# Single-tile x loads, matmul transposes, filler matmuls and a new load order at the start of a fused attention and SwiGLU kernel

## The chip, the cores and the metric

The kernel runs on one core of a Trainium2 chip. Its time is the device time of one execution in microseconds. The compute engines are PE (TensorE: matmuls), ACT (ScalarE), DVE (VectorE) and POOL (GpSimd); SP mainly issues transfers. All times in traces count from the start of the span; the quoted device times are about 1.7 us longer than the span. A run is called slow when it is over 1.5% above the fastest of the same kernel; such runs are left out of ratios.

## The reference, cut to what matters

```python
x = A_x                                             # 1 x 2048 x 512, bf16
g = sigmoid((x * gate_w).sum(-1, keepdims=True))
a = attention(x, wqkv)  @ wo                        # 32 heads of 16, causal, window of 256
b = (silu(x @ w1) * (x @ w3)) @ w2                  # F = 1376
return g * a + (1 - g) * b
```

## The kernel before

The kernel computes one static order for all engines from assumed durations and assumed landing times of the loads (the numbers in `dma(...)`), and then emits its instructions in that order. An engine works through its instructions in this order: when one waits for a load, everything behind it on that engine waits too (PE does so for 2.60 us below). A "burst" is a group of score matmuls, followed by an exp on ACT. `gate_w` is loaded as one extra column of `w1`, so that the sum for the gate comes out of the FFN matmuls.

```python
    dma("x0", "SP", 4.1, lambda: x_dma(0, 0))        # 256 tokens in one transfer
    dma("k0", "ACT", 3.6, lambda: w_dma(nc.scalar, wk_sb, A_wqkv, 0, P, D))
    dma("x1", "SP", 4.9, lambda: x_dma(0, 1))
    dma("q0", "ACT", 4.2, lambda: w_dma(nc.scalar, wq_sb, A_wqkv, 0, P))
    dma("v", "SP", 6.5, lambda: w_dma(nc.sync, wv_sb, A_wqkv, 0, D, 2 * D))
    dma("x2", "SP", 7.3, lambda: x_dma(1, 0))
    dma("x3", "SP", 8.0, lambda: x_dma(1, 1))
    dma("kq", "SP", 10.5, ...)                       # K/Q weights of the later heads
    dma("wa", "SP", 13.8, ...)                       # first part of w1 and w3
    ...                                              # [cut: x by DMA transpose, wb, w2]
    nc.gpsimd.dma_start(out=w1_sb[:, :, F:F + 1],    # gate_w: 512 elements of 2 bytes
                        in_=gate_w.rearrange("(c p x) -> p c x", p=P, x=1))
    ...
                        nc.tensor.transpose(out=tx[:, j, c, :], in_=xs_tiles[m2][:, j, d0:d0 + P],
                                            identity=ident[:])      # into bf16 PSUM
    ...
    T0, PACE, NWARM = 4.0, 2.55, 6                   # six dummy matmuls in front
```

The softmax here doesn't subtract the row's maximum and nothing guards it: scores larger than these inputs give would overflow.

Of the kernel before, what the change touches and what calls it, by code (L numbers as in the profile page):

```python
# [7 lines left out]
ALU = mybir.AluOpType  # L8
ACT = mybir.ActivationFunctionType
BF16 = mybir.dt.bfloat16  # L10
# [5 lines left out]
P = 128  # L16
# [3 lines left out]
def kernel(  # L20
# [80 lines left out]
    nc.vector.memset(scr[:], 0.0)  # L101
    xs_tiles = {}

    def x_dma(t, h):
        xs = xp.tile([P, 2, D], BF16, name=f"xs{2 * t + h}")
        nc.sync.dma_start(
            out=xs[:],
            in_=x2d[512 * t + 256 * h:512 * t + 256 * (h + 1), :].rearrange("(m p) d -> p m d", p=P))
        xs_tiles[2 * t + h] = xs

    def xt_dma(t, c):
        nc.sync.dma_start_transpose(out=xT[:, c, 512 * t:512 * (t + 1)],
# [2 lines left out]
    def w_dma(eng, dst, src, lo, hi, base=0):  # L115
        eng.dma_start(out=dst[:, :, lo:hi],
                      in_=src[:, base + lo:base + hi].rearrange("(c p) f -> p c f", p=P))
# [2 lines left out]

    land = {}

    def dma(name, eng, at, fn):
        fn()
        land[name] = at

    dma("x0", "SP", 4.1, lambda: x_dma(0, 0))
    dma("k0", "ACT", 3.6, lambda: w_dma(nc.scalar, wk_sb, A_wqkv, 0, P, D))
    dma("x1", "SP", 4.9, lambda: x_dma(0, 1))
    dma("q0", "ACT", 4.2, lambda: w_dma(nc.scalar, wq_sb, A_wqkv, 0, P))  # L130
    dma("v", "SP", 6.5, lambda: w_dma(nc.sync, wv_sb, A_wqkv, 0, D, 2 * D))
    dma("x2", "SP", 7.3, lambda: x_dma(1, 0))
    dma("x3", "SP", 8.0, lambda: x_dma(1, 1))
    dma("kq", "SP", 10.5, lambda: (w_dma(nc.sync, wk_sb, A_wqkv, P, D, D),
                                   w_dma(nc.sync, wq_sb, A_wqkv, P, D)))
    FA = 4 * P
    dma("wa", "SP", 13.8, lambda: (w_dma(nc.sync, w1_sb, B_w1, 0, FA),
                                   w_dma(nc.sync, w3_sb, B_w3, 0, FA)))
    dma("x4", "SP", 20.0, lambda: [xt_dma(2, c) for c in range(NDC)])
    dma("wb", "SP", 24.0, lambda: (w_dma(nc.sync, w1_sb, B_w1, FA, F),  # L140
                                   w_dma(nc.sync, w3_sb, B_w3, FA, F)))
    dma("x6", "SP", 30.0, lambda: [xt_dma(3, c) for c in range(NDC)])
    dma("w2", "SP", 34.0, lambda: (
        nc.sync.dma_start(out=w2_sb[:, 0:NFC - 1, :],
                          in_=B_w2[0:(NFC - 1) * P, :].rearrange("(f p) n -> p f n", p=P)),
        nc.sync.dma_start(out=w2_sb[0:FL, NFC - 1, :], in_=B_w2[(NFC - 1) * P:F, :])))
    wo_t = []

    def wo_dma():
        for j in range(2):  # L150
            wo_t.append(xp.tile([P, 2, D], BF16, name=f"xs{j}"))
            nc.sync.dma_start(out=wo_t[j][:], in_=A_wo[256 * j:256 * (j + 1), :].rearrange(
                "(c p) n -> p c n", p=P))

# [6 lines left out]
                            compare_op=ALU.is_ge, fill=0.0, base=0, channel_multiplier=1)  # L161
    nc.gpsimd.affine_select(out=eo[:], in_=eo[:], pattern=[[2 * DH, 4]],
                            compare_op=ALU.is_ge, fill=0.0, base=DH - 1, channel_multiplier=-1)
    nc.vector.tensor_reduce(out=maskEO[:, 0:1], in_=eo[:], axis=mybir.AxisListType.X, op=ALU.add)
    nc.vector.tensor_scalar(out=maskEO[:, 1:2], in0=maskEO[:, 0:1], scalar1=-1.0, scalar2=1.0,
                            op0=ALU.mult, op1=ALU.add)
    nc.gpsimd.dma_start(out=w1_sb[:, :, F:F + 1], in_=gate_w.rearrange("(c p x) -> p c x", p=P, x=1))
    nc.gpsimd.memset(Vaug[:, :, :, DH:DH + 1], 1.0)
    nc.scalar.activation(out=scr[:, 1:2], in_=scr[:, 0:1], func=ACT.Tanh)

# [23 lines left out]

    xT_op = {}

    def add_tx(m2):
        xT_op[m2] = []
        for half in range(2):
            key = ("tx", m2, half)  # L200
            hold("g", key, 1)
            cs = slice(2 * half, 2 * half + 2)

            def pe(key=key, half=half):
                tx = bank(key, BF16, (P, 2, 2, P))
                for j in range(2):
                    for c in range(2):
                        d0 = (2 * half + c) * P
                        nc.tensor.transpose(out=tx[:, j, c, :], in_=xs_tiles[m2][:, j, d0:d0 + P],
                                            identity=ident[:])  # L210

            def evac(eng, key=key, cs=cs):
                dst = xT[:, cs, 2 * m2 * P:(2 * m2 + 2) * P].rearrange("p c (j t) -> p j c t", j=2)
                if eng == "ACT":
                    nc.scalar.copy(out=dst, in_=g_tile[key][:])
                else:
                    nc.vector.tensor_copy(out=dst, in_=g_tile[key][:])

            a = Op("PE", 0.25 if m2 > 1 else 0.45, pe, [loads[f"x{m2}"]], acq=[("g", key)], kind="tx")
            xT_op[m2].append(Op("ACT" if half else "DVE", 0.55 if half else 0.36, evac, [a],  # L220
                                rel=[("g", key)], rank=-1))

    def xdep(t0, t1):
        r = []
        for m2 in range(t0 // 256, (t1 + 255) // 256):
            r += xT_op[m2] if m2 < 4 else [loads["x4" if m2 < 6 else "x6"]]
        return r

    qk_tile = {}
# [105 lines left out]
    def add_up(t, f):  # L335
        fs = fsz(f)
        has_z = f == NFC - 1
        kg, ku, kt_, kh = ("G", t, f), ("U", t, f), ("tt", t, f), ("h1", t, f)
        hold("g", kg, 2)
        hold("g", ku, 1)  # L340
        hold("tt", kt_, 1)
        hold("h1", kh, 1)
        if f == 0:
            hold("hT", t, 4)
        tl = {}

        def pe(key, wsb, d0):
            m = fs + 1 if has_z and key == kg else fs

            def fn():  # L350
                b = bank(key) if d0 == 0 else g_tile[key]
                for dc in range(d0, d0 + 1):
                    nc.tensor.matmul(b[0:m, :], lhsT=wsb[:, dc, f * P:f * P + m],  # L353
                                     rhs=xT[:, dc, t * 512:(t + 1) * 512],
                                     start=(dc == 0), stop=(dc == NDC - 1))
            return fn

        def th(eng):
            m = fs
            if has_z:  # L360
                tl["tt"] = xp.tile([P, 512], F32, name="xs2")
                m = fs + 1
            else:
                tl["tt"] = sb.tile([P, 512], BF16, name=f"tt{slot('tt', kt_)}")
            nc.scalar.activation(out=tl["tt"][0:m, :], in_=g_tile[kg][0:m, :], func=ACT.Tanh,
                                 scale=0.5)

        def s1(eng):
            tl["h1"] = sb.tile([P, 512], BF16, name=f"h1_{slot('h1', kh)}")
            nc.vector.scalar_tensor_tensor(out=tl["h1"][0:fs, :], in0=tl["tt"][0:fs, :], scalar=1.0,  # L370
                                           in1=g_tile[kg][0:fs, :], op0=ALU.add, op1=ALU.mult)

        def s2(eng):
            if t not in h_tile:
                h_tile[t] = sb.tile([P, NFC, 512], BF16, name=f"hT{slot('hT', t)}")
            nc.vector.tensor_tensor(out=h_tile[t][0:fs, f, :], in0=tl["h1"][0:fs, :],
                                    in1=g_tile[ku][0:fs, :], op=ALU.mult)

        w = loads["wa" if f < 4 else "wb"]
        x = xdep(512 * t, 512 * (t + 1))  # L380
        a0, a = pe_unit(0.87, [pe(kg, w1_sb, i) for i in range(NDC)], x + [w], acq=[("g", kg)],
                        kind="ffn")
        u0, u = pe_unit(0.87, [pe(ku, w3_sb, i) for i in range(NDC)], x + [w], acq=[("g", ku)],
                        kind="ffn")
        b = Op("ACT", 0.55, th, [a], rel=[("g", kg)], acq=[("tt", kt_)], rank=0.3)
        d = Op("DVE", 0.68, s1, [b], rel=[("g", kg), ("tt", kt_)], acq=[("h1", kh)])
        e = Op("DVE", 0.68, s2, [d, u], rel=[("g", ku), ("h1", kh)],
               acq=[("hT", t)] if f == 0 else [])
        up_done.setdefault(t, []).append(e)
        if has_z:  # L390
            add_gate(t, b, tl, fs)
        return [a0, u0]
# [175 lines left out]
        pv_out[(c, p)] = Op("SP", 2.6, tr, [b])  # L568
        return a0

    T0, PACE, NWARM = 4.0, 2.55, 6
    SEQ = []
    for p in range(NP):
        SEQ += [("d", 2 * p), ("d", 2 * p + 1)] + ([("f", p)] if p < NP - 1 else [])
# [11 lines left out]
                return n  # L586
        return per_c

    for m2 in range(4):
        add_tx(m2)  # L590
    for c in range(NDC):
        pieces = [(0, 256), (256, 512)] if c == 0 else [(0, 512)]
        pieces += [(512 * t, 512 * t + 512) for t in range(1, NTC)]
# [37 lines left out]
                d.users.append(o)  # L631
    left = {o: sum(isinstance(d, Op) for d in o.deps) for o in ops}
    free_at = {e: 0.0 for e in ("PE", "ACT", "DVE", "POOL", "SP")}
    free_at["PE"] = 3.9
    ready = {e: [] for e in free_at}
    slots = {p: [(0.0, i) for i in range(n)] for p, n in SLOTS.items()}
    count = dict(refs)
# [95 lines left out]
                    ready[x].append(u)  # L733

    with tc.manual_schedule():
        b = ps.tile([P, 512], F32, name="g0")
        for i in range(NWARM):
            nc.tensor.matmul(b[:], lhsT=warm[:, 0:P], rhs=warm[:], start=(i == 0),  # L738
                             stop=(i == NWARM - 1))
        for o in order:  # L740
            if o.kind == "burst" and not wo_t:
                wo_dma()
            if o.eng == "PE":
                o.fn()
            else:
                o.fn(o.eng)
# [30 lines left out]
```

## Time and profile before

| | |
|---|---|
| device time, 6 runs | 263.51 us median (261.43 to 264.49) |
| device time, 40 runs in the rounds with the change | 263.04 us median (260.54 to 264.98) |
| profiled execution | 263.83 us, span 262.1 us |
| last matmul ends | 258.5 us |
| PE idle, waiting for V's weights | 2.60 us at 8.0 |

The page of the kernel before starts with the span, then lists busy time, share of the span and instructions of each engine (the line goes on with the other engines):

```profile
span 262.1 us, 6553 instructions
PE 253.5 (97%) x2750; PEld 124.6 (48%) x2750; DVE 150.5 (57%) x266; ACT 195.1 (74%) x143; POOL 150.2 (57%) x251
```

PE sets the time, and whatever delays PE's stream at the start delays the end by the same amount (the second table under a3 shows it). The timeline of PE around its one large wait, kernel before. Columns: start and length in us, engine, source line, operation, output and inputs, shape, count; in brackets the idle time just before and what ended it.

```profile
5.94 1.06 PE L249 MATMUL g_165<-xT,wq_sb 128*128 128x256 bf16 x4
6.79 0.79 PE L249 MATMUL g_171<-xT,wk_sb 128*128 128x256 bf16 x4
7.42 0.60 PE L249 MATMUL g_177<-xT,wq_sb 128*128 128x256 bf16 x4
10.62 1.03 PE L294 MATMUL g_184<-edm_91,xT 128*128 128x512 bf16 x2 [2.60 <-DMA edm_91<-in_A_wqkv_dram]
11.59 0.61 PE L483 MATMUL big<-qz_164,kt_163 32*128 32x512 bf16 x4
12.14 1.03 PE L294 MATMUL g_184<-edm_91,xT 128*128 128x512 bf16 x2
```

`edm_91` holds V's weights. The first V projection starts at 10.62, after 2.60 us of nothing. The same kernel in the table of windows (busy time of PE in each stretch, granted TensorE clock, share of the DMA engines, GB/s):

```profile
core 0: us, PE busy (x), PEclk, DMA share, GB/s
6.00:8.00 2.00, 2.00 (x14) 1.00 0.79 247
8.00:10.60 2.60, 0.03 (x1) 1.00 1.08 358
10.60:14.00 3.40, 3.38 (x18) 0.50 1.10 346
14.00:20.00 6.00, 6.00 (x66) 1.00 1.29 155
```

After the idle stretch the clock is halved for one record of 3.4 us: 128x512 matmuls then start 400 to 427 ns apart instead of 215 to 216. The third view is the DMA traffic from 4 to 7 us, kernel before, in 40 slices of 75 ns (tenths of the 16 engines' time, GB/s), then packets and bytes of each queue: q1 is SP's, q10 ACT's, q0 the software queue, which carries only gate_w here.

```profile
DMA  9999999995914560240014336561854344858599
GB/s 427 362 324 290 287 280 280 277 198 123 56 24 1 1 2 0 1 1 0 27 68 109 123 109 164 150 125 68 97 109 123 137 164 150 218 177 246 205 233 233
q1 hardware_dynamic: 325, 0.32, 33.6%
q10 hardware_dynamic: 525, 0.13, 19.4%
q0 software_dynamic: 24, 0.00, 11.4%
```

From 4.8 us the engines move almost nothing, and then under 250 GB/s, although V's transfer was issued at 1.82 us.

### The profile page before, as it was taken

What the parts mean: (1) busy time and instruction counts of PE and PEld (TensorE: products, weight loads), DVE (VectorE), ACT (ScalarE), POOL (GpSimd) and SP (SyncE); (2) the same over time, 40 slices, a digit from 0 to 9 for tenths busy, and PEclk for the clock granted to TensorE, in tenths of its full rate; (3) what the DMA queues carried; (4) which work ended last, traced back from release to release, by engine and by line L of the source; (5) the groups of instructions that cost most, each with busy time, mean ns of one, the idle gap of its engine ahead of it and who ended that gap; (6) DMA issues with size and microseconds to landing.
All of it is one profiled execution on the core that took longest, in us unless ns stands there. A gap on an engine that the chain in (4) does not pass through costs nothing.

```text
span 262.1 us, 6553 instructions
## 1 busy us (share of the span) xinstructions
PE 253.5 (97%) x2750; PEld 124.6 (48%) x2750; DVE 150.5 (57%) x266; ACT 195.1 (74%) x143; POOL 150.2 (57%) x251
## 2 busy tenths in 40 slices
PE   7699999999999999999999999999999999998994
PEld 4253555544554455544454555554554454434551
DVE  2267665848647456746656458456467557446353
ACT  3287978778888887888879787798788787788400
POOL 6037575556746667556755757555756666556700
PEclk9899999999999999999999999999999999999999
DMA  5999930100000000000000000000000211101111
GB/s 140 340 177 292 318 49 9 14 10 13 11 13 10 13 10 3 13 10 13 11 13 13 11 8 10 9 10 13 14 10 13 50 48 50 41 17 54 53 50 40
DMA packets 26869, 13.05 MB, mean 50 GB/s; under 512 B 18292, under 2 KB 26836, under 8 KB 26840
## 3 DMA queue, kind: packets, MB, share of 16 engines
q1 hardware_dynamic: 25752, 12.38, 19.6%
q8 instruction: 21, 0.34, 0.6%
q10 hardware_dynamic: 1056, 0.26, 0.4%
q0 software_dynamic: 32, 0.00, 0.1%
q14 instruction: 8, 0.07, 0.1%
HBM read 7.38 MB, written 2.11 MB: 36 GB/s over the span
## 4 chain that ended last, share of the span: by engine, by line
PE 89%; DMA 5%; ACT 2%; issue 1%; DVE 1%; SPq 1%; ACTq 0%
PE big L483 11%; DMA edm_91<-in_A_wqkv_dram 3%; DMA OT<-ocur 2%; PE g_1331 L406 1%; PE g_3059 L406 1%; PE g_2201 L406 1%; PE g_4040 L406 1%; PE g_3406 L406 1%; PE g_1623 L406 1%; PE g_3188 L406 1%; PE g_2468 L406 1%; PE g_1856 L406 1%; PE g_1469 L406 1%; PE g_3683 L406 1%; PE g_2710 L406 1%; PE g_2317 L406 1%
## 5 line engine op out<-in xcount | busy, mean ns | idle before, releaser
L353 PEld LDWEIGHTS <-w_sb 128*128 128x128 bf16 (+2 forms) x352 | 31.6, 100 | 38.3 <-issue 9.1
L294 PEld LDWEIGHTS <-xT 128*128 128x128 bf16 x64 | 5.8, 98 | 9.4 <-DMA edm_91<-in_A_wqkv_dram 2.9
L434 PEld LDWEIGHTS <-OT 128*128 128x128 bf16 x64 | 5.8, 97 | 8.5 <-issue 1.5
L483 PE MATMUL big<-qz_2678,kt_2677 32*128 32x512 bf16 (+1 forms) x120 | 9.0, 329 | 0.8 <-ACT edm_3937 L491 0.6
L249 PEld LDWEIGHTS <-wq_sb 128*128 128x128 bf16 x68 | 6.5, 100 | 6.1 <-issue 0.2
L483 PE MATMUL big<-qz_164,kt_163 32*128 32x512 bf16 (+1 forms) x120 | 9.2, 336 | 0.0
L249 PEld LDWEIGHTS <-wk_sb 128*128 128x128 bf16 x68 | 6.1, 99 | 6.3 <-issue 1.1
L483 PE MATMUL big<-qz_722,kt_721 32*128 32x512 bf16 (+1 forms) x120 | 9.0, 329 | 0.0
L483 PE MATMUL big<-qz_1724,kt_1723 32*128 32x512 bf16 (+1 forms) x120 | 9.0, 329 | 0.0
L483 PEld LDWEIGHTS <-kt_2677 32*128 32x128 bf16 x120 | 2.6, 91 | 8.3 <-issue 8.0
L500 POOL TENSOR_SCALAR_AFFINE_SELECT edm_200<-edm_200 128x512 bf16<-128x512 bf16 x2 | 1.2, 645 | 9.2 <-ACT edm_200 L491 9.2
L406 PEld LDWEIGHTS <-hT_355 128*128 128x128 bf16 (+1 forms) x44 | 4.0, 98 | 5.2 <-issue 1.1
L406 PEld LDWEIGHTS <-hT_2989 128*128 128x128 bf16 (+1 forms) x44 | 4.1, 97 | 4.6
L406 PEld LDWEIGHTS <-hT_1310 128*128 128x128 bf16 (+1 forms) x44 | 3.9, 97 | 4.9 <-issue 0.9
L406 PEld LDWEIGHTS <-hT_2134 128*128 128x128 bf16 (+1 forms) x44 | 3.9, 97 | 4.7 <-issue 0.7
L483 PEld LDWEIGHTS <-kt_163 32*128 32x128 bf16 x120 | 2.4, 91 | 7.6 <-issue 7.4
L483 PEld LDWEIGHTS <-kt_721 32*128 32x128 bf16 x120 | 2.4, 91 | 7.0 <-issue 6.8
L483 PEld LDWEIGHTS <-kt_1723 32*128 32x128 bf16 x120 | 2.4, 91 | 6.9 <-issue 6.8
L491 ACT ACTIVATE edm_200<-big 128x2048 bf16<-128x2048 f32 x1 | 1.9, 1877 | 4.3 <-PE big L483 4.3
L294 PE MATMUL g_184<-edm_91,xT 128*128 128x512 bf16 x4 | 2.1, 620 | 2.6 <-DMA edm_91<-in_A_wqkv_dram 2.6
L738 PE MATMUL g_133<-warm 128*128 128x512 bf16 x6 | 2.7, 630 | 1.3 <-DVE scr L101 1.3
L505 POOL TENSOR_SCALAR_AFFINE_SELECT ef_2464<-ef_2464 128x512 bf16<-128x512 bf16 x4 | 2.4, 637 | 1.4 <-ACT ef_2464 L491 1.4
(896 smaller groups left out, 948.9 us busy)
## 6 DMA issues: line engine op xcount, KB each, us to landing
out_dram<-ot SPq DMA_DIRECT2D x16, 128.0 KB, 1.7
w_sb<-in_B_w_dram SPq DMA_DIRECT2D x2, 864.0 KB, 8.0
w_sb<-in_B_w_dram SPq DMA_DIRECT2D x1, 1280.0 KB, 6.6
w_sb<-in_B_w_dram SPq DMA_DIRECT2D x2, 512.0 KB, 8.2
OT<-ocur SPq DMA_TRANSPOSE x64, 2.3
edm_91<-in_A_wqkv_dram SPq DMA_DIRECT2D x1, 512.0 KB, 8.8
wk_sb<-in_A_wqkv_dram SPq DMA_DIRECT2D x1, 384.0 KB
wq_sb<-in_A_wqkv_dram SPq DMA_DIRECT2D x1, 384.0 KB, 10.2
```

What stands on the lines that cost most here:

```text
L249: nc.tensor.matmul(b[:, 0:n], lhsT=(wq_sb if is_q else wk_sb)[:, dc, c * P:(c + 1) * P], rhs=xT[:, dc, t0:t1], start=(dc == 0), stop=(dc = ...
L294: nc.tensor.matmul(b[:], lhsT=xT[:, c, m * P:(m + 1) * P], rhs=wv_sb[:, c, :], start=(c == 0), stop=(c == NDC - 1))
L353: nc.tensor.matmul(b[0:m, :], lhsT=wsb[:, dc, f * P:f * P + m], rhs=xT[:, dc, t * 512:(t + 1) * 512], start=(dc == 0), stop=(dc == NDC - 1))
L406: nc.tensor.matmul(b[:], lhsT=h_tile[t][0:fs, f, (m % 4) * P:(m % 4 + 1) * P], rhs=w2_sb[0:fs, f, :], start=(f == 0), stop=(f == NFC - 1))
L434: nc.tensor.matmul(b[:], lhsT=OT[:, c * S + m * P:c * S + (m + 1) * P], rhs=wo_t[c // 2][:, c % 2, :], start=(c == 0), stop=(c == NDC - 1))
L483: nc.tensor.matmul(big[:, u, k * 256:k * 256 + 2 * w], lhsT=kt[32 * u:32 * u + 32, kb * P:(kb + 1) * P], rhs=qz[32 * u:32 * u + 32, :, q0: ...
L491: nc.scalar.activation(out=e[:, :, 0:2 * n], in_=tl["big"][:, :, 0:2 * n], func=ACT.Exp, scale=SCALE)
L500: nc.gpsimd.affine_select(out=tri, in_=tri, pattern=[[0, 2], [0, 2], [1, P]], compare_op=ALU.is_ge, fill=0.0, base=0, channel_multiplier=-1)
L505: nc.gpsimd.affine_select(out=tri, in_=tri, pattern=[[0, 4], [-1, P]], compare_op=ALU.is_ge, fill=0.0, base=-1, channel_multiplier=1)
L738: nc.tensor.matmul(b[:], lhsT=warm[:, 0:P], rhs=warm[:], start=(i == 0), stop=(i == NWARM - 1))
```

## The change

The intent: begin the transposes as soon as the first 128 tokens have landed; keep PE busy until the rest lands (fillers, and transposes done as ordinary matmuls with the identity into fp32 PSUM); and take from the crowded start what is needed only later (gate_w, the K/Q weights of later heads).

```diff
-    def x_dma(t, h):
-        xs = xp.tile([P, 2, D], BF16, name=f"xs{2 * t + h}")
+    def x_dma(m0, n):
+        xs = xp.tile([P, n, D], BF16, name=f"xs{m0}")
 ...
+    dma("x0", 3.0, lambda: x_dma(0, 1))
+    dma("k0", 4.0, lambda: w_dma(nc.scalar, wk_sb, A_wqkv, 0, P, D))
+    dma("x1", 3.6, lambda: x_dma(1, 1))
+    dma("q0", 4.4, lambda: w_dma(nc.scalar, wq_sb, A_wqkv, 0, P))
+    dma("x2", 4.7, lambda: x_dma(2, 2))
+    dma("v", 6.6, lambda: w_dma(nc.sync, wv_sb, A_wqkv, 0, D, 2 * D))
+    dma("x4", 7.4, lambda: x_dma(4, 2))
+    dma("x6", 8.1, lambda: x_dma(6, 2))
+    dma("wa", 11.4, ...)           # kq now stands behind x12, before w2
 ...
-    nc.gpsimd.dma_start(out=w1_sb[:, :, F:F + 1], in_=gate_w...)   # now gate_dma(), at the 8th burst
-    nc.vector.tensor_reduce(out=maskEO[:, 0:1], ...)               # now three small ops on POOL
 ...
-    nc.tensor.transpose(out=tx[:, j, c, :], in_=..., identity=ident[:])
+    nc.tensor.matmul(tx[:, c - c0, :], lhsT=xs_tiles[m][:, c * P:(c + 1) * P],
+                     rhs=ident[:], start=True, stop=True)
+    if m < 2 and c1 == NDC:
+        warm_up(1 + m)             # one filler behind tile 0, two behind tile 1
 ...
-    T0, PACE, NWARM = 4.0, 2.55, 6
+    T0, PACE, NWARM = 4.0, 2.55, 4
 ...                                # [cut: evacuations in halves for tiles 0 and 1; wo also at the 8th burst]
```

More of the change, by code (lines that the diff above doesn't have):

```diff
@@ L102 @@
     xs_tiles = {}
-    def x_dma(t, h):
-        xs = xp.tile([P, 2, D], BF16, name=f"xs{2 * t + h}")
+    def x_dma(m0, n):
+        xs = xp.tile([P, n, D], BF16, name=f"xs{m0}")
         nc.sync.dma_start(
-            out=xs[:],
-            in_=x2d[512 * t + 256 * h:512 * t + 256 * (h + 1), :].rearrange("(m p) d -> p m d", p=P))
-        xs_tiles[2 * t + h] = xs
+            out=xs[:], in_=x2d[P * m0:P * (m0 + n), :].rearrange("(m p) d -> p m d", p=P))
+        for j in range(n):
+            xs_tiles[m0 + j] = xs[:, j, :]
     def xt_dma(t, c):
@@ L121, with dma @@
     land = {}
-    def dma(name, eng, at, fn):
+    def dma(name, at, fn):
         fn()
         land[name] = at
-    dma("x0", "SP", 4.1, lambda: x_dma(0, 0))
-    dma("k0", "ACT", 3.6, lambda: w_dma(nc.scalar, wk_sb, A_wqkv, 0, P, D))
-    dma("x1", "SP", 4.9, lambda: x_dma(0, 1))
-    dma("q0", "ACT", 4.2, lambda: w_dma(nc.scalar, wq_sb, A_wqkv, 0, P))
-    dma("v", "SP", 6.5, lambda: w_dma(nc.sync, wv_sb, A_wqkv, 0, D, 2 * D))
-    dma("x2", "SP", 7.3, lambda: x_dma(1, 0))
-    dma("x3", "SP", 8.0, lambda: x_dma(1, 1))
-    dma("kq", "SP", 10.5, lambda: (w_dma(nc.sync, wk_sb, A_wqkv, P, D, D),
-                                   w_dma(nc.sync, wq_sb, A_wqkv, P, D)))
-    FA = 4 * P
-    dma("wa", "SP", 13.8, lambda: (w_dma(nc.sync, w1_sb, B_w1, 0, FA),
-                                   w_dma(nc.sync, w3_sb, B_w3, 0, FA)))
-    dma("x4", "SP", 20.0, lambda: [xt_dma(2, c) for c in range(NDC)])
-    dma("wb", "SP", 24.0, lambda: (w_dma(nc.sync, w1_sb, B_w1, FA, F),
-                                   w_dma(nc.sync, w3_sb, B_w3, FA, F)))
-    dma("x6", "SP", 30.0, lambda: [xt_dma(3, c) for c in range(NDC)])
-    dma("w2", "SP", 34.0, lambda: (
+    dma("x0", 3.0, lambda: x_dma(0, 1))
[6 more added lines that the diff above has]
+    dma("x6", 8.1, lambda: x_dma(6, 2))
+    FA = 4 * P
+    dma("wa", 11.4, lambda: (w_dma(nc.sync, w1_sb, B_w1, 0, FA),
+                             w_dma(nc.sync, w3_sb, B_w3, 0, FA)))
+    dma("x8", 17.0, lambda: [xt_dma(2, c) for c in range(NDC)])
+    dma("wb", 23.0, lambda: (w_dma(nc.sync, w1_sb, B_w1, FA, F),
+                             w_dma(nc.sync, w3_sb, B_w3, FA, F)))
+    dma("x12", 28.0, lambda: [xt_dma(3, c) for c in range(NDC)])
+    dma("kq", 31.0, lambda: (w_dma(nc.sync, wk_sb, A_wqkv, P, D, D),
+                             w_dma(nc.sync, wq_sb, A_wqkv, P, D)))
+    dma("w2", 35.0, lambda: (
         nc.sync.dma_start(out=w2_sb[:, 0:NFC - 1, :],
@@ L147, with gate_dma @@
     wo_t = []
+    def gate_dma():
+        nc.gpsimd.dma_start(out=w1_sb[:, :, F:F + 1],
+                            in_=gate_w.rearrange("(c p x) -> p c x", p=P, x=1))
     def wo_dma():
         for j in range(2):
-            wo_t.append(xp.tile([P, 2, D], BF16, name=f"xs{j}"))
+            wo_t.append(xp.tile([P, 2, D], BF16, name=f"xs{2 * j + 2}"))
             nc.sync.dma_start(out=wo_t[j][:], in_=A_wo[256 * j:256 * (j + 1), :].rearrange(
@@ L163 @@
                             compare_op=ALU.is_ge, fill=0.0, base=DH - 1, channel_multiplier=-1)
-    nc.vector.tensor_reduce(out=maskEO[:, 0:1], in_=eo[:], axis=mybir.AxisListType.X, op=ALU.add)
-    nc.vector.tensor_scalar(out=maskEO[:, 1:2], in0=maskEO[:, 0:1], scalar1=-1.0, scalar2=1.0,
+    nc.gpsimd.tensor_tensor(out=eo[:, 0:2], in0=eo[:, 0:2], in1=eo[:, 2:4], op=ALU.add)
+    nc.gpsimd.tensor_tensor(out=maskEO[:, 0:1], in0=eo[:, 0:1], in1=eo[:, 1:2], op=ALU.add)
+    nc.gpsimd.tensor_scalar(out=maskEO[:, 1:2], in0=maskEO[:, 0:1], scalar1=-1.0, scalar2=1.0,
                             op0=ALU.mult, op1=ALU.add)
-    nc.gpsimd.dma_start(out=w1_sb[:, :, F:F + 1], in_=gate_w.rearrange("(c p x) -> p c x", p=P, x=1))
     nc.gpsimd.memset(Vaug[:, :, :, DH:DH + 1], 1.0)
@@ L195, with warm_up, add_tx, pe @@
     xT_op = {}
-    def add_tx(m2):
-        xT_op[m2] = []
-        for half in range(2):
-            key = ("tx", m2, half)
-            hold("g", key, 1)
-            cs = slice(2 * half, 2 * half + 2)
-            def pe(key=key, half=half):
-                tx = bank(key, BF16, (P, 2, 2, P))
-                for j in range(2):
-                    for c in range(2):
-                        d0 = (2 * half + c) * P
-                        nc.tensor.transpose(out=tx[:, j, c, :], in_=xs_tiles[m2][:, j, d0:d0 + P],
-                                            identity=ident[:])
-            def evac(eng, key=key, cs=cs):
-                dst = xT[:, cs, 2 * m2 * P:(2 * m2 + 2) * P].rearrange("p c (j t) -> p j c t", j=2)
+    def warm_up(n):
+        b = ps.tile([P, 4, 512], F32, name="big")
+        for i in range(n):
+            nc.tensor.matmul(b[:, 0, :], lhsT=warm[:, 0:P], rhs=warm[:], start=(i == 0),
+                             stop=(i == n - 1))
+    def add_tx(m):
+        xT_op[m] = []
+        halves = [(0, 2), (2, 4)] if m < 2 else [(0, 4)]
+        for n, (c0, c1) in enumerate(halves):
+            key = ("tx", m, c0)
+            hold("g", key, 1)
+            def pe(key=key, c0=c0, c1=c1):
+                tx = bank(key, shape=(P, c1 - c0, P))
+                for c in range(c0, c1):
+                    nc.tensor.matmul(tx[:, c - c0, :], lhsT=xs_tiles[m][:, c * P:(c + 1) * P],
+                                     rhs=ident[:], start=True, stop=True)
+                if m < 2 and c1 == NDC:
+                    warm_up(1 + m)
+            def evac(eng, key=key, c0=c0, c1=c1):
+                dst = xT[:, c0:c1, m * P:(m + 1) * P]
                 if eng == "ACT":
@@ L217, in evac @@
                     nc.vector.tensor_copy(out=dst, in_=g_tile[key][:])
-            a = Op("PE", 0.25 if m2 > 1 else 0.45, pe, [loads[f"x{m2}"]], acq=[("g", key)], kind="tx")
-            xT_op[m2].append(Op("ACT" if half else "DVE", 0.55 if half else 0.36, evac, [a],
-                                rel=[("g", key)], rank=-1))
+            src = loads[f"x{m if m < 2 else m - m % 2}"]
+            a = Op("PE", (0.11 if m < 4 else 0.058) * (c1 - c0) + 0.43 * (1 + m) * (m < 2 and c1 == NDC), pe, [src], acq=[("g", key)],
+                   kind="tx")
+            on_act = n == 1 or (len(halves) == 1 and m % 2 == 1)
+            xT_op[m].append(Op("ACT" if on_act else "DVE", 0.36 if len(halves) == 2 else 0.66, evac,
+                               [a], rel=[("g", key)], rank=-1))
     def xdep(t0, t1):
         r = []
-        for m2 in range(t0 // 256, (t1 + 255) // 256):
-            r += xT_op[m2] if m2 < 4 else [loads["x4" if m2 < 6 else "x6"]]
+        for m in range(t0 // P, (t1 + P - 1) // P):
+            r += xT_op[m] if m < 8 else [loads["x8" if m < 12 else "x12"]]
         return r
@@ L360, in th @@
             if has_z:
-                tl["tt"] = xp.tile([P, 512], F32, name="xs2")
+                tl["tt"] = xp.tile([P, 512], F32, name="xs6")
                 m = fs + 1
@@ L587, in first_use @@
         return per_c
-    for m2 in range(4):
-        add_tx(m2)
+    for m in range(8):
+        add_tx(m)
     for c in range(NDC):
@@ L633 @@
     free_at = {e: 0.0 for e in ("PE", "ACT", "DVE", "POOL", "SP")}
-    free_at["PE"] = 3.9
+    free_at["PE"] = 3.0
     ready = {e: [] for e in free_at}
@@ L735 @@
     with tc.manual_schedule():
-        b = ps.tile([P, 512], F32, name="g0")
-        for i in range(NWARM):
-            nc.tensor.matmul(b[:], lhsT=warm[:, 0:P], rhs=warm[:], start=(i == 0),
-                             stop=(i == NWARM - 1))
+        warm_up(NWARM)
         for o in order:
-            if o.kind == "burst" and not wo_t:
+            if o is burst_ops[7]:
                 wo_dma()
+                gate_dma()
             if o.eng == "PE":
```

## The prediction

> **What bounds the kernel.** TensorE. The page gives PE 97% of a 262.1 us span; the table of windows shows PE 40.0 of every 40 us from 20 to 180; the chain of waits is 89% PE. ACT is busy 74%, DVE 57%, POOL 57%. Time without PE is at the ends: 3.6 us of draining after the last matmul (258.5), about 1 us of small waits between 220 and 250, and the start.
>
> **The start (timeline of PE, windows).** Six dummy matmuls 1.26 to 4.00, transposes from 4.15, first Q/K projections to 8.02, then PE stands still 2.60 us until V's weights land (10.58; issued 1.82, 8.76 us on the way). The groups name that DMA as the releaser. Then the granted clock is 0.50 from 10.6 to 13.9: 128x512 matmuls start 427 ns apart there, 216 ns afterwards. The Trainium skill, "TensorE: Matmul & The Clock Gate", Part 1, says that an idle window of about 3.4 us halves the clock; this trace agrees (one 3.41 us record at 0.5 after the stall). Loss: half of 3.3 us = 1.65. Matmuls before about 7.1 us also run at the slow spacing; that stays.
>
> Why V is late: all DMA engines go nearly empty from 4.6 to 5.5 and carry 50 to 250 GB/s until 7, then 340 to 370. In that stretch the 32 packets of the software queue (gate_w, 2-byte elements) run[...]. The skill's "DMA: Bandwidth & Descriptors", Specifications, says that transfers under 512 B are read-modify-write, below line rate. I think gate_w holds the engines up; the trace shows coincidence, not cause.
>
> **What the change does.**
> - It removes gate_w from the start. The bytes ahead of V are the same 768 KB, so V should land about 7 (estimate: 768 KB done by 5.0 as now, 512 KB at 340 GB/s = 1.5 us, plus 0.4): the 2.6 us stall mostly goes, and the slow-clock window, 1.65 us. Sum about 4.2.
> - The first x tile is half the size: transposes start near 3.1, not 4.15 (-1.05). But three fillers at 427 ns now stand behind it (+1.28). Net +0.2 to +0.4.
> - Transposes become ordinary matmuls with fp32 results: same 107/56 ns spacing, but evacuating 512 columns rises from 0.41 to about 0.69 us on DVE (as for V). Those engines have room.
> - K/Q weights of later heads move behind x and FFN weights: FFN weights land about 2 us sooner; later heads need theirs only after 35 us. Off the critical path. wo and gate_w move to the eighth burst, needed much later.
> - After about 18 us the PE stream is the same work, shifted; the static order is recomputed, perhaps ±0.5 us.
>
> Gain: 2.6 + 1.65 - 0.4 - 0.5 (leftover stalls on V or FFN weights) = about 3.3 us: 263.5 becomes 260.2 us, 1.3% less. Range 258.3 to 262.3. Chances: faster by over 2% 0.12, within 2% 0.86, slower 0.02.
>
> **What would show it.** PE timeline: no wait over 0.5 us on V's weights; V landing at 6.5 to 7.5; no clock record of 0.5 after 7 us; transposes from about 3.1; first burst at 7.5 to 8.5, not 11.6; first FFN matmul (19.7 now) about 3 us earlier; steady state unchanged; DMA not empty near 5 us.
>
> **What would make it wrong.** V still late because descriptors, not gate_w, open the gap (gain then 1 to 2 us); FFN weights landing after the schedule's 11.4 and stalling PE; POOL blocked by the gate_w issue in the middle of the masks; or a clock window so phased that the start warms up sooner (gain up to 5 us).

## The result, and the profile after

| | before | after |
|---|---|---|
| median | 263.04 us (40 runs) | 261.49 us (20 runs) |
| range | 260.54 to 264.98 | 260.91 to 264.31 |
| ratio of fast runs | | 0.9978, 95% interval 0.9954 to 1.0003: the same |
| profiled execution | 263.83 us | 260.30 us |

A ratio is the mean time of one kernel's fast runs over that of the other's of the same rounds, so it is not quite the ratio of the medians. The time lies inside the predicted range, but the forecast was a gain of 1.3% and the measured one is 0.2%. Three later samples of the same kernel gave 0.9963, 0.9935 and 0.993, so the gain is somewhere between 0.2 and 0.7%, still about half of the forecast at best.

The profile of after seemed to say the opposite. Its page, its timeline of PE and its windows:

```profile
span 258.6 us, 6559 instructions
```

```profile
5.93 0.48 PE L218 MATMUL g_166<-ident,xs_98 128*128 128x128 bf16 x4
6.25 0.60 PE L263 MATMUL g_174<-xT,wq_sb 128*128 128x256 bf16 x4
6.68 0.60 PE L263 MATMUL g_180<-xT,wk_sb 128*128 128x256 bf16 x4
7.16 0.82 PE L308 MATMUL g_186<-edm_91,xT 128*128 128x512 bf16 x3
7.91 0.40 PE L497 MATMUL big<-qz_173,kt_172 32*128 32x512 bf16 x4
```

```profile
8.00:10.60 2.60, 2.27 (x25) 1.00 1.09 359
10.60:14.00 3.40, 3.40 (x21) 1.00 1.15 179
```

There is no wait for V, no halved clock, and the span is 3.5 us shorter than that of before. Both profiles are single draws, though: before's execution (263.83) was 0.9 us slower than its mean of 262.92, and after's (260.30) was faster than every one of the 20 timed runs. Two profiles from opposite sides of two scatters made 3.5 us out of a difference of 0.8 us between the means.

### The profile page after: what moved, and what is told of

The parts are those of the page before. It is cut to its first block, busy times and chain, and to the rows that moved or that the text cites. A ratio compares the mean times of both kernels' runs of the same rounds, so it can differ in the third digit from the quotient of the medians.

```text
span 258.6 us, 6559 instructions
## 1 busy us (share of the span) xinstructions
PE 252.0 (97%) x2751; PEld 123.9 (48%) x2751; DVE 150.4 (58%) x265; ACT 195.3 (76%) x144; POOL 150.7 (58%) x254
## 4 chain that ended last, share of the span: by engine, by line
PE 87%; ACT 6%; POOL 2%; issue 1%; DVE 1%; DMA 1%; SPq 0%; POOLq 0%; ACTq 0%
PE big L497 11%; PE g_4064 L420 1%; PE g_3417 L420 1%; PE g_3988 L420 1%; PE g_3684 L420 1%; PE g_3200 L420 1%; PE g_2465 L420 1%; PE g_2153 L420 1%; PE g_2719 L420 1%; PE g_2337 L420 1%; PE g_1483 L420 1%; PE g_1335 L420 1%; PE g_1853 L420 1%; PE g_1619 L420 1%; PE g_4093 L420 1%
## 5 line engine op out<-in xcount | busy, mean ns | idle before, releaser
L263 PEld LDWEIGHTS <-wq_sb 128*128 128x128 bf16 x68 | 5.9, 97 | 5.9 <-issue 1.4
L205 PE MATMUL big<-warm 128*128 128x512 bf16 x7 | 3.6, 629 | 1.3 <-DVE scr L101 1.3
L514 POOL TENSOR_SCALAR_AFFINE_SELECT edm_203<-edm_203 128x512 bf16<-128x512 bf16 x2 | 1.2, 643 | 5.7 <-ACT edm_203 L505 5.7
L519 POOL TENSOR_SCALAR_AFFINE_SELECT ef_654<-ef_654 128x512 bf16<-128x512 bf16 x4 | 2.4, 634 | 1.5 <-ACT ef_654 L505 1.5
L519 POOL TENSOR_SCALAR_AFFINE_SELECT ef_2484<-ef_2484 128x512 bf16<-128x512 bf16 x4 | 2.4, 635 | 1.4 <-ACT ef_2484 L505 1.4
L519 POOL TENSOR_SCALAR_AFFINE_SELECT ef_279<-ef_279 128x512 bf16<-128x512 bf16 x4 | 2.4, 635 | 1.4 <-ACT ef_279 L505 1.4
```

The source lines that it names most:

```text
L205: nc.tensor.matmul(b[:, 0, :], lhsT=warm[:, 0:P], rhs=warm[:], start=(i == 0), stop=(i == n - 1))
L263: nc.tensor.matmul(b[:, 0:n], lhsT=(wq_sb if is_q else wk_sb)[:, dc, c * P:(c + 1) * P], rhs=xT[:, dc, t0:t1], start=(dc == 0), stop=(dc = ...
L514: nc.gpsimd.affine_select(out=tri, in_=tri, pattern=[[0, 2], [0, 2], [1, P]], compare_op=ALU.is_ge, fill=0.0, base=0, channel_multiplier=-1)
L519: nc.gpsimd.affine_select(out=tri, in_=tri, pattern=[[0, 4], [-1, P]], compare_op=ALU.is_ge, fill=0.0, base=-1, channel_multiplier=1)
```

## The experiments

All kernels gave correct results. Each was timed in five rounds beside the kernel before on its own chip; four kernels went to a chip together, so the groups below (a1, a2, e1, e2; e3 to e6; e7 to e9 with a3; f1, f2, f4, a4) share a chip and its runs of before. The result raised two theories: A, that V's lateness in before is a matter of luck, and B, that it is there in every execution and the change gives its value back elsewhere.

### a1, a2: both kernels again

> The kernel before, unchanged. Ratio 1.000 to itself within 0.3%. Its times should fall again in two groups, near 261.5 and near 263.6. Theory A (the late V is a matter of luck: gate_w's small packets delay V only in some executions, and the profile of before fell in one): a second profile shows V landing at another time, a stall between 0 and 2.6 us, and a profile of the 261.5 group has a stall under 1 us. Theory B (V is late in every execution of before, and the two groups come from the phase of the clock window): V lands at 10 to 11 us again, stall 2.3 to 2.9 us, whatever the group.

Measured: ratio 0.9963 (interval 0.9906 to 1.002); before against itself and just outside the expected 0.3%, so this is the size of the noise. The profile (262.99 us) shows a wait for V of 1.82 us instead of 2.60, V at 9.94, and again a halved clock. V and the wait fall just short of what B expected (10 to 11, 2.3 to 2.9 us) and inside A's wider range, so this run alone decides nothing.

Theory B put the two groups of times down to the clock, and the record bears it out. Each run lists its mean clock, and one halved record of 3.41 us takes about 0.0065 off a mean over 262 us (estimate: half of 3.41 over 262). Of the 50 runs of before in these experiments, 21 list 0.997 or more (mean 261.82 us), 24 list 0.991 to 0.993 (263.46) and five 0.985 or 0.986 (264.92); the first two groups overlap a little (up to 262.81, from 262.61). So a halved record costs about 1.6 us, and 21 of 50 executions had none.

> The kernel after, unchanged. Ratio to before 0.997 +- 0.002. Both theories: no wait for V, V landing near 7. Theory A: a profile of its slower group (263.5) would show some other wait or slow clock at the start of about 2 us. Theory B: the slower group shows the clock going full one or two windows later, with no wait.

Measured: 261.66 us, 0.9963 (0.9912 to 1.0013). The profile has waits where the first one had none: 0.57 us for x tiles 2 and 3, 0.36 us for V, which landed at 8.46. The first part of the expectation, V near 7, failed.

### e1: only gate_w moves

```diff
 # before
-    nc.gpsimd.dma_start(out=w1_sb[:, :, F:F + 1], in_=gate_w...)
 ...
+            if o is burst_ops[7]:
+                nc.gpsimd.dma_start(out=w1_sb[:, :, F:F + 1], in_=gate_w...)
```

> Before, with only the load of gate_w moved from the start to the eighth burst. Theory A: V lands at 6.5 to 7.5 in the profile, times mostly in the 261.5 group, ratio 0.995 to before. Theory B: the same landing, but ratio 0.984 to 0.990 (stall and slow window gone in every execution), so faster than the whole change, which then gives about 2 us back elsewhere (fillers, fp32 evacuations, order). Rival C (gate_w has nothing to do with it, the gap comes from descriptors): V still lands after 9.5, ratio 1.000.

Measured: 259.66 us (259.35 to 260.03), 0.9873 (0.9827 to 0.9919). One moved load is 3.3 us faster than before (means 259.65 and 262.98) and 2.4 us faster than the whole change on that chip (262.01). The timeline of PE of e1, same columns as above:

```profile
5.92 1.06 PE L248 MATMUL g<-xT,wq_sb 128*128 128x256 bf16 x4
6.77 0.70 PE L248 MATMUL g<-xT,wk_sb 128*128 128x256 bf16 x4
7.31 0.60 PE L248 MATMUL g<-xT,wq_sb 128*128 128x256 bf16 x4
7.75 0.59 PE L293 MATMUL g<-edm,xT 128*128 128x512 bf16 x2
```

This is the stream of before without the hole. Nor is the clock halved (windows, columns as above):

```profile
8.00:10.60 2.60, 2.49 (x26) 1.00 1.11 330
10.60:14.00 3.40, 3.40 (x28) 1.00 1.15 330
```

The DMA traffic from 4 to 7 us in e1 has no hole either:

```profile
DMA  9999999999999999989999999999999999999999
GB/s 393 335 311 287 304 260 287 311 317 321 287 283 273 232 246 246 341 259 369 369 328 341 300 369 369 341 355 314 369 341 369 328 355 341 369 341 369 341 355 301
```

The trace also keeps the semaphore updates of each transfer. The Trainium skill, "DMA: Bandwidth & Descriptors", section "Why a DMA increments its semaphore by 16 and not by 1", says that each engine that takes part in a transfer adds its own 1 when its data is there; the traces agree, with 16 updates for every load at the start. So one can see how far apart the engines finish (us; the updates of each transfer in order of time, since the trace does not name the engines):

| transfer | first | 8th | 15th | last |
|---|---|---|---|---|
| gate_w, before | 5.98 | 6.66 | 7.97 | 9.14 |
| V, before | 7.48 | 8.04 | 9.32 | 10.58 |
| x behind V, before | 8.18 | 8.76 | 10.05 | 11.32 |
| V, e1 | 6.73 | 6.89 | 7.05 | 7.10 |

In before, V's arrivals follow gate_w's at 1.3 to 1.8 us, from the first to the last, as if each engine had to end its share of gate_w before its share of V; the spread of 3.1 us is handed on to the next transfer. Without gate_w the sixteen arrivals lie within 0.37 us. That gate_w is the cause, where the prediction had only a coincidence, is shown by the moved load; how the two queues share an engine is read from the order of the arrivals alone. Nor is it shown what in this load holds the engines up. Its own packets took only 11.4% of the engines' time in the view of 4 to 7 us above; for most of the hole the trace shows the engines doing nothing. Its sixteen packets of 64 bytes took 185 to 775 ns each in before, and 44 ns each when e1 ran the same load at 29 us. e1 moved the 2-byte pieces and the software queue together; gate_w on SP's or ACT's queue at the start would have told them apart, and was not run.

### e2: the change with gate_w put back

```diff
 # after
+    gate_dma()
     nc.gpsimd.memset(Vaug[:, :, :, DH:DH + 1], 1.0)
 ...
                 wo_dma()
-                gate_dma()
```

> After, with only the load of gate_w put back at the start. Theory A: V late in some executions only, ratio 0.999 to before. Theory B: V lands after 9.5, a stall of 2 us or more, ratio 1.005 to 1.010 (slower than before by the fillers). Rival C: V lands near 7 as in after, ratio 0.997.

Measured: 265.03 us, 1.0073 (1.0024 to 1.0123), slower than before. V landed at 10.13; already x tiles 2 and 3 were late (8.02), PE waited 2.56 us for them, and the clock was halved afterwards. Timeline of PE of e2:

```profile
8.06 0.62 PE L219 MATMUL g<-ident,xs 128*128 128x128 bf16 x8 [2.56 <-DMA xs<-in_A_x_dram]
8.52 0.95 PE L264 MATMUL g<-xT,wq_sb 128*128 128x256 bf16 x4
```

Theory B holds (every run of before was slower than every run of e1): gate_w is worth 3 us from either side, and everything else in the change together costs about 2.

### e3 to e6: one part of the rest undone at a time

No sample of after ran on this chip, so "like after" compares ratios to before with those of other chips.

Fillers all in front, as before (the order stays that of after):

```diff
 # after
-                if m < 2 and c1 == NDC:
-                    warm_up(1 + m)
-    T0, PACE, NWARM = 4.0, 2.55, 4
+    T0, PACE, NWARM = 4.0, 2.55, 6
```

> After, with the three fillers behind tiles 0 and 1 taken out and six dummy matmuls at the front as before (order otherwise the same). The question is where the change gives back the 2.2 us by which before with gate_w moved alone (259.66) beats it (about 261.9). Theory F (fillers stand in the critical PE stream, 3 x 427 ns): ratio to before 0.991 to 0.993, about 1.2 us faster than after. Theory D (x tiles 2 and 3 and V land later than with paired loads): PE just waits where the fillers stood, ratio 0.996 to 0.998, within 0.4 us of after, wait for x of 1 us or more in the profile.

Measured: 261.83 us, 0.9968 (0.9925 to 1.001), like after. PE stood where the fillers had been, waiting for x tiles 2 and 3. Timeline of PE of e3:

```profile
3.79 1.06 PE L218 MATMUL g<-ident,xs 128*128 128x128 bf16 x8
6.91 0.62 PE L218 MATMUL g<-ident,xs 128*128 128x128 bf16 x8 [2.06 <-DMA xs<-in_A_x_dram]
```

Tiles 0 and 1 in one transfer:

```diff
 # after
-    dma("x0", 3.0, lambda: x_dma(0, 1))
+    dma("x0", 3.0, lambda: x_dma(0, 2))
-    dma("x1", 3.6, lambda: x_dma(1, 1))
+    land["x1"] = 3.6
+    dma("x2", 4.7, lambda: x_dma(2, 2))     # moved here from behind q0
```

> After, with tiles 0 and 1 loaded in one transfer as before, tiles 2 and 3 issued right behind it (one issue earlier). Static order the same as after. Theory D: tiles 2 and 3 land by about 5, V by 7.8, no wait for x over 0.2 us after the fillers, ratio 0.988 to 0.991, and the slower group of after near 263.5 disappears. Theory F: no better than after, 0.996 to 1.000 (the first transposes start 0.7 us later).

Measured: 261.96 us, 0.9962 (0.9919 to 1.0005), like after, so theory D alone failed. Tiles 2 and 3 did land early (5.21), but now the fillers stood in front of their transposes. Timeline of PE of e4:

```profile
5.26 1.06 PE L205 MATMUL big<-warm 128*128 128x512 bf16 x2
6.11 0.99 PE L218 MATMUL g<-ident,xs 128*128 128x128 bf16 x8
6.94 0.60 PE L263 MATMUL g<-xT,wq_sb 128*128 128x256 bf16 x4
```

Transposes as before (bf16 results), instruction for instruction the same order:

```diff
 # after
-                tx = bank(key, shape=(P, c1 - c0, P))
+                tx = bank(key, BF16, (P, c1 - c0, P))
-                    nc.tensor.matmul(tx[:, c - c0, :], lhsT=..., rhs=ident[:], start=True, stop=True)
+                    nc.tensor.transpose(out=tx[:, c - c0, :], in_=..., identity=ident[:])
```

> After, with PE transposes into bf16 in place of matmuls with the identity into fp32, everything else the same instruction for instruction. Theory M (the fp32 evacuations delay the projections): evacuations of 512 columns fall from 0.69 to 0.42 us on DVE, the 0.21 us wait for xT goes, ratio 0.003 or more below after's 0.9965. Theories D and F: within 0.15% of after. If transposes do not count as activity for the clock, the clock would be granted later and the kernel up to 1 us slower.

Measured: 261.41 us, 0.9957 (0.991 to 1.0005). The 0.21 us wait for xT went, as expected; the time is not distinguishable from after's. The first clock record, at full speed, begins at 5.5 us, within the 4.5 to 7.0 of the four profiles of after, so no delay of the clock by transposes showed.

K/Q weights of the later heads in front of the FFN weights again:

```diff
 # after
+    dma("kq", 31.0, ...)    # moved back up, before wa
```

> After, with the K/Q weights of the later heads issued before the FFN weights again, as in before. Compute order the same as after. Theories D and F: within 0.2% of after (0.9965), because those weights stand behind x and V either way and the FFN weights, about 2 us later (near 14), are first used at 17 to 18.6 us. If FFN weights were what after waits for, this would be slower by 1 us or more.

Measured: 261.30 us, 0.9943 (0.9901 to 0.9985), not distinguishable from after. No wait for FFN weights appeared in its profile.

### e7, e8, e9: the two delays together, and the load sizes

e7 is e3 and e4 in one.

> After, with both undone at once that changed nothing each alone: tiles 0 and 1 in one transfer, and no fillers behind the tiles (six dummy matmuls in front). In e3 the first projection waited for x tiles 2 and 3 (7.37), in e4 for the fillers (6.94). Theory J (two events in parallel delay the first projection, and taking one away uncovers the other): the first projection starts near 6.0, ratio to before 0.988 to 0.991, most of the 2.2 us back. Rival S (the recomputed static order is what costs): projection near 6.0 but ratio still 0.995 to 0.997.

Measured: 260.66 us, 0.9914 (0.9871 to 0.9956), against 261.23 for after on the same chip. The first projection starts at 5.65, as theory J wanted, but only about 0.5 us came back (means 260.75 and 261.22). Now PE waited 1.53 us for V: it asked for V at 6.69 and V landed at 8.18 (this profile fell on e7's slowest run). Timeline of PE of e7:

```profile
8.22 0.82 PE L306 MATMUL g<-edm,xT 128*128 128x512 bf16 x3 [1.53 <-DMA edm<-in_A_wqkv_dram]
```

e8 moves the Q weights of the first heads from the ACT queue to the SP queue:

```diff
 # after
-    dma("q0", 4.4, lambda: w_dma(nc.scalar, wq_sb, A_wqkv, 0, P))
     dma("x2", 4.7, lambda: x_dma(2, 2))
+    dma("q0", 4.4, lambda: w_dma(nc.sync, wq_sb, A_wqkv, 0, P))
```

> After, with the Q weights of the first heads moved from the ACT queue to the SP queue, behind x tiles 2 and 3. Theory D2 (with x in small transfers the SP queue runs short, so that the ACT queue's weights take the engines first and x tiles 2 and 3 land late): x tiles 2 and 3 land before 5.5, no wait for x, first projection at 6.2 to 6.5, V 7.2 to 8; ratio 0.989 to 0.993. If the late x has another cause: x still lands after 6, ratio 0.996.

Measured: 261.50 us, 0.9941 (0.9899 to 0.9984), like after. Tiles 2 and 3 landed at 5.73, inside after's own range (5.43 to 6.30) and later than in three of its four profiles, and V at 8.47. Theory D2, that the ACT queue's weights push x back, is not supported.

e9 takes e1 and cuts its first two x loads into four:

```diff
 # e1
-        nc.sync.dma_start(out=xs[:], in_=x2d[...256 rows...].rearrange("(m p) d -> p m d", p=P))
+        for j in range(2):                   # for the first 512 tokens only
+            r = 512 * t + 256 * h + P * j
+            nc.sync.dma_start(out=xs[:, j, :], in_=x2d[r:r + P, :])
```

> e1 (before with gate_w late, 259.66, ratio 0.987), with the first two x loads each cut into two transfers of one token tile; nothing else, compute order the same. Theory D2: tiles 2 and 3 land 0.5 to 1.5 us later than e1's 5.1, the first projection starts near 6.4 to 7.2 instead of 5.9, ratio 0.990 to 0.994, with more spread. If cutting the loads is harmless: ratio 0.987 as e1, spread 0.7 us.

Measured: 261.23 us (260.46 to 261.92), 0.9934 (0.9893 to 0.9974), against e1's 0.9873 and 0.9867 on two other chips. The cut loads cost about 1.6 us (0.006 to 0.007 in the ratio); the order of the computation is e1's. Tiles 2 and 3 landed at 5.75 instead of 5.05, and V at 9.11 instead of 7.10, for one engine's sake: the fifteenth arrival was at 7.39. One thing changed with the cut: SP has two more transfers to issue ahead of V, which was issued at 2.66 instead of 1.82. V's first arrival was no later for that (6.46, against 6.73 in e1). Timeline of PE of e9:

```profile
9.16 0.61 PE L297 MATMUL g<-edm,xT 128*128 128x512 bf16 x2 [1.54 <-DMA edm<-in_A_wqkv_dram]
```

### a3: after again

> After, unchanged, third sample. Ratio 0.9965 +- 0.003. Two of three executions near 261.4, one of three near 263.4. Where the profile falls in the slower group, theory D2 expects x tiles 2 and 3 or V one to two us later than in the others (V after 9), possibly with a granted clock of 0.5 afterwards; where it falls in the faster group it looks like the first two profiles (x tiles 2 and 3 at 5.4 to 6.4, V at 7 to 8.5).

Measured: 261.23 us (260.77 to 261.79), 0.9935 (0.9896 to 0.9975); no run in the slower group. The timeline of PE in its profile shows what the first profile of after happened not to show:

```profile
5.68 0.62 PE L218 MATMUL g<-ident,xs 128*128 128x128 bf16 x8 [0.47 <-DMA xs<-in_A_x_dram]
6.13 0.60 PE L263 MATMUL g<-xT,wq_sb 128*128 128x256 bf16 x4
6.57 0.60 PE L263 MATMUL g<-xT,wk_sb 128*128 128x256 bf16 x4
8.75 0.82 PE L308 MATMUL g<-edm,xT 128*128 128x512 bf16 x3 [1.58 <-DMA edm<-in_A_wqkv_dram]
```

Compare e1's lines above. After asks for V at 7.17, right behind the first Q and K projection; e1 does another Q projection first and asks at 7.75. V's last arrival here was 8.71 (the fifteenth at 7.39). At that moment the second Q projection was ready, but it stood behind V in PE's order.

Two regularities come out of the profiles so far. First, the spread of V's sixteen arrivals, last minus first, without gate_w at the start. The later runs f1, f2, f4 and a4 are included; a load counts as cut when tiles 0 and 1 come in two transfers.

| first x loads | spread of V's arrivals, us | V's last arrival, us |
|---|---|---|
| 256 tokens (e1, f1, e4, f4, e7) | 0.37, 0.45, 0.73, 1.03, 1.49 | 7.10 to 8.18 |
| 128 tokens (after, a4, e6, e5, e3, e8, f2, a2, a3, e9) | 0.67, 1.25, 1.62, 1.78, 1.79, 1.80, 2.03, 2.18, 2.40, 2.65 | 7.11 to 9.11 |

The two ranges overlap, and each value is one execution. Second, the time from the start of the first V projection to the end of the last matmul, both from the timeline:

| kernel | first V projection | last matmul ends | difference |
|---|---|---|---|
| after | 7.16 | 254.91 | 247.75 |
| a2, a3, a4 | 8.51, 8.75, 7.72 | 256.25, 256.44, 255.41 | 247.74, 247.69, 247.69 |
| e1, f1 | 7.75, 7.79 | 254.40, 254.39 | 246.65, 246.60 |
| e9 | 9.16 | 255.95 | 246.79 |

Behind the first V projection everything runs as if on rails. The execution time is V's start plus a constant, and the constant is 0.9 to 1.1 us larger in after's order than in before's, because less of the other work is done by then. The second half of the Q projection (four matmuls at 109 ns, 0.44 us) and 0.32 us of waits at the next transposes and their evacuation account for most of it.

### f2, f4: the same transfers, another order

The order is computed from assumed landing times. The change assumes V at 6.6; its last arrivals were 7.11, 8.46, 8.71 and 7.68 in the four profiles of after.

```diff
 # after
-    dma("x2", 4.7, ...    +    dma("x2", 5.6, ...
-    dma("v", 6.6, ...     +    dma("v", 8.6, ...
-    dma("x4", 7.4, ...    +    dma("x4", 9.4, ...
-    dma("x6", 8.1, ...    +    dma("x6", 10.1, ...
```

With these numbers PE's order has both halves of Q and K and a first burst in front of V. Not one transfer or computation differs from after.

> After, with only the assumed landing times of four loads changed for the static order (x tiles 2 and 3 4.7 to 5.6, V 6.6 to 8.6, x4 7.4 to 9.4, x6 8.1 to 10.1; about what the traces of after show). Transfers and instructions are the same, their order is not: both halves of Q, K and a first burst now stand ahead of V. Theory O (the order asks for V too early, and the other ready work stands behind the wait): wait for V under 0.4 us, time from the first V projection to the last matmul falls from 247.7 to 246.7 or less, ratio to before 0.989 to 0.992. Rival (late data as such is what costs, the order is harmless): ratio as after, 0.9935 to 0.9965.

Measured: 259.58 us median, 0.9862 (0.9829 to 0.9896), against 261.24 for after (a4) on the same chip; the means are 260.04 and 261.29. The recorded ratio, below the expected 0.989 to 0.992, fits the mean of the four faster runs (259.52); with the fifth (262.14) it would be 0.988. Theory O holds, the rival falls: four assumed times are worth 1.3 us in the mean and 1.7 us in the median, most of the 1.64 us by which after trails e1 on that chip.

Its profile fell on its slowest run (262.14; the other four 258.95 to 260.40), and shows where a slower group can come from. First its timeline of PE, then its windows:

```profile
7.11 0.62 PE L218 MATMUL g<-ident,xs 128*128 128x128 bf16 x8 [1.95 <-DMA xs<-in_A_x_dram]
7.57 0.73 PE L263 MATMUL g<-xT,wq_sb 128*128 128x256 bf16 x4
11.31 1.03 PE L308 MATMUL g<-edm,xT 128*128 128x512 bf16 x4
```

```profile
8.00:11.30 3.30, 3.30 (x18) 0.50 1.57 352
```

The last engine brought tiles 2 and 3 at 7.07 (the fourteenth had at 5.55), PE idled for 1.95 us, and the clock was halved for the 3.4 us that followed. V, last at 8.49, was there long before PE asked. From V's start to the end it is 245.47 us, less than the 246.7 expected; but more of the other work now stands ahead of V, so this number alone shows no gain.

> f2, and besides tiles 0 and 1 in one transfer and no fillers behind the tiles (e7). Theory O and D together: as good as before with gate_w late, ratio 0.986 to 0.989. If the order does nothing: as e7, 0.9914.

Measured: 259.62 us median, 0.9863 (0.9827 to 0.9898), from three fast runs (259.33 to 259.78). The profiled run was slow (264.88 us, granted clock 0.948 from start to end), so its times are not compared. With undivided loads and no fillers the new order is no faster than f2, but none of its three fast runs was late.

### f1, a4: e1 and after side by side again

> e1 again (before with gate_w moved to the eighth burst). Ratio 0.987 +- 0.002, spread of the executions under 1 us, V's sixteen arrivals within 0.3 to 1 us of each other, last at 7.0 to 7.8, no wait for V over 0.3 us.

Measured: 259.66 us (259.52 to 259.75), 0.9867 (0.9837 to 0.9897).

> After again, beside e1 on the same chip: 1.5 to 2.5 us slower than it, ratio to before 0.993 to 0.998; V's sixteen arrivals 0.7 to 2.5 us apart, last at 7.1 to 8.8 in the faster group; if the profile falls in the slower group (263.5), V later than 9 or x tiles 2 and 3 later than 7, or the granted clock back at 0.5 after the wait.

Measured: 261.24 us (260.77 to 261.94), 0.993 (0.9903 to 0.9956). On this chip the single moved load beats the whole change by 1.64 us (means 259.65 and 261.29); on the first chip it was 2.36. e1 beats both kernels with one moved load; f2 and f4 come as low on this chip.

## Why the prediction was wrong

- **PE bounds the kernel, and the start is what can be gained.** Right. From the first V projection on, the four profiles of after agree within 0.06 us.
- **gate_w holds up V.** Right, and now shown: e1 took V's last arrival from 10.58 to 7.10, e2 put it back to 10.13. The Trainium skill's "DMA: Bandwidth & Descriptors", Specifications, states read-modify-write and less than line rate for transfers under 512 B. No run here shows the read-modify-write, and slow packets alone do not explain the hole (their 11.4%, see e1). The cost was the up to 3 us that each engine came late with everything queued behind it; whether the small pieces or the software queue did it stays open.
- **The stall and the halved clock are worth 4.2 us.** Too large by 0.9: e1 gained 3.3. The sum was read from one profile, which was 0.9 us slower than the mean and had a halved record. The size of one was right (about 1.6 us between the groups under a1), but 21 of 50 executions had none, so on average it was worth 1.1 us; the executions without one (mean 261.82) were 2.2 us slower than e1, and 2.2 and 1.1 make the 3.3. The skill's "TensorE: Matmul & The Clock Gate", Part 1, has the clock halve after an idle window of about 3.4 us. The records at half clock were 3.41 us long, but here shorter waits were enough: in before, a1, e2 and f2 a wait of 1.8 to 2.6 us was followed by one record of 0.5. It need not be: e3's wait of 2.06 us was not followed by one, so the price of such a wait differs from execution to execution.
- **Fillers cost 0.2 to 0.4 net.** Not confirmed as a cost of their own: taking them out (e3) changed nothing measurable, because x tiles 2 and 3 were the next to be late. With the loads paired (e4) they did stand in the way. Each hid the other; e7 took both away.
- **fp32 evacuations and K/Q weights are off the critical path.** Right for the weights (e6), within the noise. The evacuations seem to cost about 0.3 us: from V's start to the end e5's profile has 247.43 us, against 247.69 to 247.75 in after; the timed runs can't tell this from nothing.
- **"The bytes ahead of V are the same 768 KB, so V should land about 7."** This step failed for the changed kernel. It is right for e1 and f1 (7.10, 7.37), but in after a transfer's arrivals were spread over more time, and it has landed only with its last engine: V at 7.11 to 8.71. e9 shows that cutting the first loads costs 1.6 us. That the spread comes from the cut is likely, not shown: e7, uncut, had V at 8.18.
- **"The static order is recomputed, perhaps ±0.5 us", and 0.5 us of leftover stalls.** This is the term that was mis-sized most. What the rest of the change gives back, counted as 0.9 in the prediction (0.4 and 0.5), measured 1.6 to 2.4 us (after against e1). The order asks for V at 7.2, on the assumption of 6.6, with ready work behind it; f2, which differs in nothing but the order, recovers 1.3 us in the mean. In all, the prediction's sum was 4.2 - 0.9 = 3.3; measured, it was 3.3 for gate_w less 1.6 to 2.4 for the rest. That gate_w alone gives the very 3.3 us that were forecast for the whole is a coincidence.

What stays open: why cut loads scatter the engines' arrivals. e8 speaks against the share that the ACT queue takes; the later issue that comes with more transfers (e9) and other causes were not isolated. Also open is the slower group of after itself (262.7 to 264.3 in 7 of its first 20 runs): f2's profile shows one way into such a time, but no profile of after fell in that group, and only one of those runs lists a mean clock low enough for a whole halved record (0.992).

## What to carry to other kernels

Look for the smallest transfer in the crowded start first: one kilobyte, in 2-byte pieces on the software queue, delayed half a megabyte by 2.6 to 3.5 us (before and a1 against f1 and e1), and moving it alone gave more than the whole rearrangement. When a static order is computed from assumed landing times, take the last arrivals of several profiles and lean to the late side; an order that asks early puts ready work behind a wait. And don't read the size of a gain of 1% from one profile of each kernel: see first where the profiled runs lie among the timed ones.

## What the Trainium skill lacked or had wrong

- "DMA: Bandwidth & Descriptors" says that small transfers are below line rate, but gives no figure for what they cost transfers on other queues: V's arrivals followed those of gate_w (32 packets, up to 775 ns each) by 1.3 to 1.8 us, and V's last arrival came 3.5 us later than without it (10.58 in before, 7.10 in e1).
- The same page does not say how the arrivals of a transfer scatter over the engines when the loads before it are cut in two: last minus first was 0.37 to 1.49 us behind loads of 256 KB, and 0.67 to 2.65 us behind loads of 128 KB, one execution each.
- "TensorE: Matmul & The Clock Gate", Part 4, says that transpose mode does not count as busy for the clock in the same way. No cost of that showed, though other matmuls ran beside the transposes: with transposes in place of matmuls (e5) the clock was full at 5.5 us, and the median was 261.41, against 261.23 to 261.66 in four samples of after.
- "TensorE: Matmul & The Clock Gate", Part 1, asks for an idle window of about 3.4 us: waits of 1.82 to 2.60 us were followed by a record at half clock in four profiles (before, a1, e2, f2), and one of 2.06 us was not (e3).
- No page says that the profile's clock row shows 1.00 before the first record, while the matmuls still start 427 ns apart, as they did before about 7.1 us in the kernel before.
